# A gated sum of an FFT filter and a Mish layer on one core: first x tiles moved up, small dummy products, the plain rows of W in two transfers, and a new order

## The chip, the cores and the metric

The kernel runs on one core of a Trainium2 chip. A core has TensorE (PE, matrix products into PSUM), VectorE (DVE), ScalarE (ACT), GpSimd (POOL) and SyncE (SP, here the issuer of nearly all DMA transfers), and 16 DMA engines that carry the transfers. The metric is the device time of one execution in microseconds, the median of several runs.

## The reference: what is computed

`x` is 2048 x 512. Two branches read it, and a gate per row mixes them:

```python
g = sigmoid((x * gate_w).sum(-1, keepdims=True))
a = irfft2(rfft2(x) * (w_r + 1j * w_i), s=(2048, 512))     # w: 2048 x 257
h = x @ w1 + b1                                            # w1: 512 x 1792
b = (h * tanh(softplus(h))) @ w2                           # Mish, w2: 1792 x 512
out = g * a + (1 - g) * b                                  # bf16
```

## The kernel before, in words

`x` is held as 16 tiles of 128 rows (row `16 p + t` is partition `p` of tile `t`). Both branches are written as products with a 128 x 128 or 128 x 512 moving side on TensorE.

*The dense branch.* It needs `x` transposed. Tiles 0 to 7 are transposed by TensorE (`tr0` to `tr7`, line 562) and copied out of PSUM (`evx`); tiles 8 to 15 by transposing DMAs (`xt8` to `xt15`, line 462). The rows go in four chunks c of four tiles. `m{c}_{ft}` (line 866) is a group of four products of 512 columns for one of 14 slices of w1; ACT applies Mish as it empties the bank (`h{c}_{ft}`, line 871). `n{t}` (line 884) is 14 products with w2 for tile t; `o{t}` scales it by 1 - g.

*The FFT branch*, a chain of products with constant matrices: sum and difference of the halves of x (`bf`, line 575, DVE or POOL), `p0` to `p15` (line 588) with evacuations `ep`, `d0` to `d15` (line 603) with `ed`, then a re-layout through 16 SBUF-to-SBUF transfers `s{fq}_{r}` (rE<-rD), then `t{q}_{i}` (line 718, needs `s` of its quarter and the constants `ldM`) with evacuations `et`. The filter is `p1`, `p2`, `ad` on DVE with copies `sw` (swapped halves); a correction of the edge frequencies (`e1`, `xp`, `es`, `ead`, `e2`, `e3`); the inverse chain `it`, `eit`, eight transfers `hx`, `id`, `ec`, `ey`, and `ip`, `fin`, which add it to the other branch. `gate0`, `gate8`, `zcl`, `ez`, `omg`, `zt` and the like compute the gate.

*The weights W of the filter.* For the real part (`wr`) and the imaginary part (`wi`) the 2048 x 257 rows go into the staging tile `rS`. The frequencies are paired with their mirror images: plain rows go forward (`wr0s0`, `wr1s0`, `wi0s0`, `wi1s0`, 16 runs of 16,448 bytes each), mirrored rows one by one backward (`...s1`, runs of 514 bytes; `...s2` a single row of each). The copies `wrm...`, `wim...` (lines 644, 645), `wrn`, `win`, `wrc`, `wrz` (and `wi...`) unfold them into `rW` and `rA`. `rS` is later reused for Mish results of chunk 3.

*The order.* Nothing loops: each step is a task, and the string `ORDER` (line 326) lists all tasks. An entry is name, engine where there is a choice, and buffer numbers (PSUM banks or `tmp` slots). Each engine issues its tasks strictly in that order; `emit` puts the semaphore waits ahead of each instruction. The DMA tasks are SP's, and SP issues them in order as well (`braw`, `graw` and the last output are on ACT's queue). A task that waits holds all that stand behind it on its engine. The string came from a planner that used the durations given with the tasks (the numbers in `dma(...)` and `G.add(...)`); at run time these numbers do nothing.

*The start.* `warm` (line 509) is 13 products of 256 columns on a constant, with no input. The bytes of the first transfers decide when `tr`, `bf`, `p` and the first `m` can run.

Of the kernel before, what the change touches and what calls it, by code (L numbers as in the profile page):

```python
# [346 lines left out]
ec0:dve:0 id3 n0_0::7 ec2:act:1 ey0_0 ey0_1 ey2_0 ey2_1 id4::4 o0_0:act ip0::0 id10::2 id11 ip1::1 fin0 ec10:act:1 id14::6 id15 id5 fin1 ec14:act:0
n6_0::0 ec4:act:2 ey10_0 out1 ey14_0 ey14_1 ey10_1 ey4_1 id8::6 o6_0:act id9 id6::2 ey4_0 n11_0::1 ec8:act:1 ey8_1 ey8_0 ip3::0 ip11_0 fin3 id7
o11_0:act n14_0::6 ec6:act:1 ey6_1 ey6_0 ip7::7 ip14_0 id12::2 o14_0:dve n4_0::1 out14 ip6::6 o4_0:act n10_0::0 fin6 ip10_0 ip2::6 o10_0:act ip4::1
fin2 n7_0::4 out11 fin4 out3 n15_256::6 o7_0:act fin7 ip15_256 id13 out7 o15_256:act n8_0::7 ec12:dve:1 out15_256 ey12_1 ey12_0 ip8_0 n13_0::6 o8_0:act  # L350
ip13_0 n12_0::7 o13_0:act ip12_0 n9_0::6 o12_0:act out13 ip9_0 ip5::7 o9_0:act n15_0::2 fin5 out9 out5 ip15_0 o15_0:act out15_0
"""


def _build(nc, A_x, A_w_r, A_w_i, B_x, B_w1, B_b1, B_w2, gate_w, out, merge=8, xtp=8, NWARM=13):
# [4 lines left out]
    d_M = nc.inline_tensor(_bf16_bits(cs["M"]), name="c_m").bitcast(BF)  # L360
    d_G = nc.inline_tensor(_bf16_bits(cs["G"]), name="c_g").bitcast(BF)
    scz = nc.dram_tensor("scz", (NT, 128), BF)

    G = _Graph(3)
    es = ExitStack()
    with es:
# [61 lines left out]
        def bank(b, i=0):  # L428
            return ps[:, b.slot + i, :]
# [27 lines left out]
        def dma(name, dst, src, us, cls="dma", queue="sp", is_out=False, transpose=False, **kw):  # L457
            def fn(e, _dst=dst, _src=src):
                a = _dst() if callable(_dst) else _dst
                b = _src() if callable(_src) else _src  # L460
                if transpose:
                    return e.dma_start(a, b, transpose=True)  # L462
                return e.dma_start(a, b)  # L463
# [40 lines left out]
        wb = _Buf("b1")  # L504
# [467 lines left out]
```

## Time and profile before

| | us |
|---|---|
| median of 3 runs (range) | 137.81 (137.18 to 137.94) |
| the profiled execution's time | 137.92 |
| its span, first to last instruction | 136.2 |
| TensorE (PE) busy | 127.2 (93%) |
| DVE, ACT, POOL busy | 77.6, 76.7, 13.1 |
| bytes moved | 20.41 MB, 150 GB/s over the span |

The page names groups of instructions by line, engine, operation and tile; "idle before" is the time in which the engine had nothing to run just before an instruction, with what ended it. `PEclk` and the clock column of a table of windows give the granted clock of TensorE as a share of full speed. The columns of such a table are: the stretch, its length, busy time of PE, PEld (weight loads), DVE, ACT and POOL with the number of instructions, the clock, the share of time that the 16 DMA engines were busy, and GB/s. In lists of waits the numbers are us in total, times, and the longest. A DMA line gives how many issues, KB each, and us from issue to landing; a queue line gives packets, MB, and share of the 16 engines' time. A timeline line gives start, length, engine, line, operation, tiles and count; lines on SP are the time that it takes SP to issue.

### The profile page before, as it was taken

The numbers are of one execution on the slowest core, as the hardware profiler recorded it, in microseconds if no ns is written. First come the engines' busy times: TensorE is split into PE (matmuls) and PEld (weight loads), VectorE is DVE, ScalarE is ACT, GpSimd is POOL, SyncE is SP. The second block draws the span as 40 slices with busy tenths as digits, with TensorE's granted clock in tenths as the row PEclk, the third lists the DMA queues.
The fourth block names the chain that finished last, engine by engine and source line by source line (L and its number), as shares of the span: only waits on it lengthen the run. The fifth ranks groups of instructions, "written<-read, shape, count | busy, mean of one in ns | idle before, by whom it ended". The sixth has DMA issues, their size and how long they took to land.

```text
span 136.2 us, 2309 instructions
## 1 busy us (share of the span) xinstructions
PE 127.2 (93%) x902; PEld 71.2 (52%) x918; DVE 77.6 (57%) x129; ACT 76.7 (56%) x107; POOL 13.1 (10%) x21
## 2 busy tenths in 40 slices
PE   7499999999998699999989999999999999999992
PEld 5295577654564255444536664466554444744451
DVE  0474669575699989998952458036975224340020
ACT  4067889897798789999977910232433022312221
POOL 3032045403400000000040000000000000000000
PEclk9959999999999999999999999999999999999999
DMA  4999999996876899579923100780200102220024
GB/s 119 317 244 278 162 379 240 331 146 149 197 172 136 182 170 207 114 236 346 386 79 104 56 0 0 279 338 2 82 0 0 39 0 80 79 96 0 0 77 173
DMA packets 15710, 20.41 MB, mean 150 GB/s; under 512 B 5780, under 2 KB 11796, under 8 KB 15636
## 3 DMA queue, kind: packets, MB, share of 16 engines
q1 hardware_dynamic: 15520, 20.20, 55.3%
q8 instruction: 7, 0.11, 0.4%
q10 hardware_dynamic: 180, 0.07, 0.2%
q14 instruction: 3, 0.02, 0.1%
HBM read 12.92 MB, written 2.10 MB: 110 GB/s over the span
## 4 chain that ended last, share of the span: by engine, by line
PE 56%; ACT 13%; SPq 12%; DMA 11%; DVE 3%; issue 2%; POOLq 1%
PE ps L884 35%; SPq L463 10%; PE ps L866 10%; DMA rS<-in_A_w_r_dram 8%; DMA rX<-in_A_x_dram 3%; ACT rD L871 3%; ACT rW L665 3%; PE ps L840 3%; PE ps L796 3%; ACT rD L496 2%; SPq L462 2%; ACT hs L871 2%; DVE rC L742 1%; PE ps L892 1%; PE ps L910 1%
## 5 line engine op out<-in xcount | busy, mean ns | idle before, releaser
L866 PE MATMUL ps<-rX,w_sb 128*128 128x512 bf16 x215 | 50.9, 380 | 2.0 <-DMA rX<-in_A_x_dram 1.2
L866 PEld LDWEIGHTS ps<-rX,w_sb 128*128 128x128 bf16 x224 | 20.9, 98 | 23.4 <-issue 2.1
L898 ACT ACTIVATE rX<-ps,omg 128x512 bf16<-128x512 f32 (+1 forms) x14 | 9.2, 657 | 42.3 <-PE ps L884 23.8
L884 PE MATMUL ps<-w_sb,hs 128*128 128x512 bf16 x108 | 24.8, 379 | 0.2
L871 ACT ACTIVATE hs<-ps,b1f 128x512 bf16<-128x512 f32 x28 | 18.9, 690 | 3.0 <-PE ps L866 2.7
L914 DVE SCALAR_TENSOR_TENSOR rX<-ps,gcol,rX 128x512 bf16<-128x512 f32 x8 | 5.8, 748 | 21.5 <-PE ps L910 17.9
L884 PEld LDWEIGHTS ps<-w_sb,hs 128*128 128x128 bf16 x112 | 10.7, 98 | 12.1
L884 PE MATMUL ps<-w_sb,rS 128*128 128x512 bf16 (+1 forms) x70 | 12.9, 336 | 0.0
L496 ACT ACTIVATE rC<-ps 128x1024 bf16<-128x1024 f32 x12 | 12.2, 1032 | 1.1 <-PE ps L718 0.7
L884 PE MATMUL ps<-w_sb,rD 128*128 128x512 bf16 x53 | 12.3, 379 | 0.2
L851 DVE TENSOR_TENSOR rA<-tmp,ps 128x512 bf16<-128x512 f32 x16 | 10.0, 682 | 1.1 <-ACT tmp L847 1.1
L871 ACT ACTIVATE rS<-ps,b1f 128x512 bf16<-128x512 f32 x14 | 9.3, 697 | 1.9 <-PE ps L866 1.9
L871 ACT ACTIVATE rD<-ps,b1f 128x512 bf16<-128x512 f32 x14 | 9.1, 692 | 1.7 <-PE ps L866 1.6
L884 PEld LDWEIGHTS ps<-w_sb,rS 128*128 128x128 bf16 x70 | 6.8, 98 | 5.5
L884 PEld LDWEIGHTS ps<-w_sb,rD 128*128 128x128 bf16 x56 | 5.4, 98 | 6.1
L575 DVE TENSOR_TENSOR rB<-rA 128x1024 bf16<-128x1024 bf16 (+1 forms) x8 | 4.8, 637 | 6.3 <-DMA rA<-in_A_x_dram 6.3
L728 DVE COPY tmp<-rC 64x1024 bf16<-64x1024 bf16 x15 | 6.2, 421 | 1.6 <-ACT tmp L729 0.7
L588 PE MATMUL ps<-w_sb,rB 128*128 128x128 bf16 x64 | 5.5, 246 | 0.1
L493 DVE CAST rC<-ps 128x1024 bf16<-128x1024 f32 x4 | 4.9, 1218 | 1.3 <-PE ps L588 0.7
L493 DVE CAST rF<-ps 128x1024 bf16<-128x1024 f32 x4 | 4.7, 1218 | 1.3 <-PE ps L796 1.3
L742 DVE TENSOR_TENSOR rC<-rC,tmp 128x1024 bf16<-128x1024 bf16 x8 | 5.3, 688 | 0.1
L496 ACT ACTIVATE rX<-ps 128x512 bf16<-128x512 bf16 x4 | 2.4, 595 | 5.3 <-PE ps L562 5.3
(84 smaller groups left out, 133.6 us busy)
## 6 DMA issues: line engine op xcount, KB each, us to landing
w_sb<-in_B_w_dram SPq DMA_DIRECT2D x3, 768.0 KB, 9.7
rF<-c_m SPq DMA_DIRECT2D x4, 512.0 KB, 13.7
rE<-rD SPq DMA_DIRECT2D x16, 128.0 KB, 2.3
rB<-c_g SPq DMA_DIRECT2D x4, 512.0 KB, 7.1
out_dram<-rX SPq DMA_DIRECT2D x7, 256.0 KB, 2.1
rA<-in_A_x_dram SPq DMA_DIRECT2D x3, 512.0 KB, 7.6
rC<-rF SPq DMA_DIRECT2D x4, 384.0 KB, 3.0
w_sb<-in_B_w_dram SPq DMA_DIRECT2D x2, 512.0 KB, 9.5
```

Of the source, the lines that this page charges most:

```text
L463: return e.dma_start(a, b)
L493: return e.tensor_copy(out=o(), in_=i())
L496: return e.activation(o(), i(), AF.Copy)
L588: ins = e.matmul(bank(b, i)[:, 128 * c:128 * (c + 1)], xu[:, t, uv, e_:256:2], RF, start=True, stop=True)
L728: G.add(f"sw{q}_{j}", [("dve", 0.37, lambda e, z=z, lo=lo, i_=i_: e.tensor_copy(out=tb(z)[lo:lo + 64], in_=i_)), ("act", act(1024), lambda ...
L742: return e.tensor_tensor(out=Y[:, fa:fb, :], in0=Y[:, fa:fb, :], in1=zv(z), op=ALU.add)
L851: return e.tensor_tensor(out=yb[:, t:t + 2, 256 * h:256 * h + 256].rearrange("p t (i e) -> p t i e", e=2), in0=t4(z), in1=o4(bank(b, 1)), ...
L866: ins = e.matmul(bank(b), w1_sb[:, dt_, 128 * ft:128 * (ft + 1)], xT[:, c, dt_, :, :], start=(dt_ == 0), stop=(dt_ == 3))
L871: G.add(f"h{c}_{ft}", [("act", act(512, 1), lambda e, c=c, ft=ft, b=b: e.activation(hs[c][:, ft, :], bank(b), AF.Mish, bias=b1f[:, ft:ft + ...
L884: ins = e.matmul(bank(b)[:, 0:hi - lo], hs[c][:, ft, 128 * tl:128 * (tl + 1)], w2_sb[:, ft, lo:hi], start=(ft == 0), stop=(ft == NFT - 1 a ...
L898: return e.activation(bs[:, t, lo:hi], bank(b)[:, 0:hi - lo], AF.Copy, scale=omg[:, t:t + 1])
L914: return e.scalar_tensor_tensor(out=bs[:, t, :], in0=bank(b), scalar=gcol[:, t:t + 1], in1=bs[:, t, :], op0=ALU.mult, op1=ALU.add)
```

## The change

Four things, and a new `ORDER` for all tasks:

- The transfer of tiles 0 and 1 (`x0`) is the first on SP, `x2` the second; `x4` was first.
- 14 new tasks `fl0` to `fl13`, each two products of 128 columns on the same constant and PSUM bank as `warm`, without inputs; they stand among the first transposes and `p` products.
- The plain rows of W come in one transfer for each of `wr` and `wi` (`wrs0`, `wis0`) of 32 rows of 16,448 bytes, to every second partition of 64, in place of two of 16 rows each. The mirrored rows stay as they were.
- Some planner durations of DMA tasks are other numbers.

Lines after the insertion are 8 higher than before (562 becomes 570, 718 becomes 726, 866 becomes 874).

```diff
 ORDER = """
-warm::0 braw wrp1 x4 ones lut ident wrp0 cRF ebase graw x0 w1_0 tr7::0 bf4_1:dve x2 tr4::1 bf4_0:dve tr5::2 wi0s0 evx4:dve tr0::3 bf0_1:pool evx5:dve
-tr_b::1 evx7:dve p6::4 evx0:act wr0s2 p7 ev_b p4::6 bf0_0:dve tr6::3 x12 ep6:dve p5 evx6:act p0::0 p1 tr1::2 ep4:act m1_3::3 ep0:dve bf2_0:pool x8
-evx1:act tr2::6 m1_1::7 h1_3 bf2_1:dve wr0s0 evx2:act p2::2 p3 h1_1 tr3::6 m1_0::0 ep2:act evx3:dve wr0s1 bf12_0:dve m0_3::1 h1_0 bf12_1:dve m1_2::2
-h0_3 bf8_0:dve w1_4 bf8_1:dve p14::6 h1_2 p15 p12::0 m0_0::3 wip1 ep14:act wip0 cFD p8::4 ldM2 h0_0 p9 gate0::6 ep8:act wrm010:dve p13 p10::2 ldM1 zcl0
-wrm000:pool ep12:dve p11 m0_2::4 ep10:act m0_7::5 wi0s1 h0_2 wrm001:dve d4::2 h0_7 d5 d10::0 wrm011:dve d11 ed4:act d0::6 ldM3 d1 ed10:dve m0_6::5 ez0
-ed0:act d2::2 m1_4::4 ldM0 wrn0:dve h0_6 m1_7::6 h1_4 ez10 w1_8 wrc0:dve d3 omg0 wrz0:pool h1_7 d8::4 ezb0 gc0 d9 m1_6::7 ed2:act d6::0 ed8:act d7
-m0_4::6 wi0s2 ed6:dve h1_6 xt12 d14::4 d15 h0_4 d12::2 d13 ed14:act m1_5::0 ed12:dve xt9 m0_5::1 h1_5 wim001:dve s0_1 m1_10::2 h0_5 wim011:dve s3_2
-m0_9::3 wim010:dve s0_3 h1_10 s0_2 m1_8::1 wim000:pool h0_9 s0_0 m1_12::0 h1_8 s1_1 s2_1 m0_8::3 h1_12 win0:dve s2_3 m1_11::2 h0_8 s1_3 t1_0::0
-wic0:pool s1_0 h1_11 t1_1 t0_0::4 wiz0:pool et1:dve s1_2 t0_1 m0_10::3 et0:act xt10 m0_13::2 sw1_0:dve:0 h0_10 sw0_0:dve:1 s3_1 m0_11::4 sw0_1:dve
-h0_13 sw1_1:dve s2_0 p2_0:dve t3_0::0 h0_11 t3_1 s2_2 t2_0::2 p2_1:dve t2_1 et3:act m1_9::5 xt8 p1_1:dve et2:act p1_0:dve m0_12::4 xt11 sw3_1:dve:2
-h1_9 t4_0::0 ad_0:dve t4_1 t5_0::2 h0_12 t5_1 sw3_0:dve m1_13::5 s3_0 sw2_1:dve:1 et5:act sw2_0:dve s3_3 m0_1::4 p1_3:dve et4:act wr1s1 p1_2:dve
-m2_6::2 h0_1 p2_2:dve h1_13 m2_8::3 wr1s0 p2_3:dve h2_6 ad_2:dve t7_0::4 m2_2::0 h2_8 wi1s0 ad_3:dve sw4_0:dve:1 t7_1 h2_2 m2_12::3 sw4_1:dve wi1s1
-sw5_0:dve:2 et7:act m2_1::2 sw5_1:dve ad_1:dve h2_12 t6_0::4 m2_0::0 sw7_0:dve:0 h2_1 ldG3 wrm111:dve t6_1 h2_0 m2_3::2 sw7_1:dve wrm100:dve rft
-et6:act m2_10::3 wrm101:dve xt14 h2_3 m2_7::4 wrm110:dve h2_10 xt15 wim110:dve wrn1:act m2_11::5 wim100:dve m2_13::3 xt13 wim111:dve m2_5::2 wim101:dve
-w2_8 m2_4::0 win1:dve m2_9::1 h2_11 wrc1:dve h2_4 wic1:dve inv m3_8::6 h2_9 wiz1:dve wrz1:pool ldG0 p1_5:dve m3_4::5 h2_13 p1_4:dve h3_8 ldG1 m3_2::3
-p2_4:dve h2_7 p2_5:dve m3_7::6 h3_4 edge ad_4:dve h3_2 m3_1::7 p2_7:dve w2_2 sw6_0:act:1 p1_7:dve m3_11::3 h3_1 sw6_1:dve m3_13::5 ad_7:dve h3_11
-p1_6:dve ldG2 h2_5 m3_3::7 p2_6:dve h3_13 gate8::2 h3_3 ad_5:dve h3_7 m3_9::3 ad_6:dve zcl8 e1::6 ez8 m3_10::2 h3_9 xp1::1 ezb8 es0::2 ez18 zt::3
...
+warm::0 lut ebase x0 ones wrp1 x2 wrp0 ident braw cRF graw w1_0 fl0 fl1 fl2 fl3 bf0_1:dve tr1::1 ldM2 tr0::2 bf0_0:dve evx1:act fl4 fl5 evx0:dve fl6
+fl7 bf2_0:pool tr3::3 fl8 tr_b::2 fl9 evx3:act p0::4 ev_b p1 x4 tr2::1 bf2_1:dve ep0:act fl10 fl11 fl12 evx2:dve fl13 p2::2 p3 m0_3::1 ep2:act w1_4
+m0_2::0 h0_3 m0_0::2 h0_2 ldM0 m0_1::3 h0_0 bf4_0:dve cFD tr4::0 bf4_1:dve h0_1 tr6::1 tr7::2 x12 tr5::4 evx4:dve p6::6 evx7:dve p7 m0_5::0 evx6:dve
+ep6:act evx5:dve x8 p4::2 p5 h0_5 m1_7::6 ep4:act ldM1 m1_1::7 h1_7 m1_5::2 h1_1 bf12_1:dve w1_8 m1_4::3 bf12_0:dve h1_5 gate0::7 h1_4 bf8_0:dve p14::0
+bf8_1:dve p15 p12::2 zcl0 ep14:act p13 wrs0 wip0 p10::4 p11 ez0 p8::6 ep12:act p9 m1_3::0 ez10 wip1 ep8:dve wr0s1 ep10:act m1_2::1 omg0 ezb0 h1_3 gc0
+d0::4 d1 h1_2 d10::6 d11 wi0s1 d8::2 ed0:act m0_13::0 ed10:act m1_12::1 h0_13 wr1s1 d4::4 d5 d6::6 h1_12 ed4:dve d7 d9 ed6:act m1_8::0 wr0s2 d14::4
+ed8:act d15 d12::6 xt10 ed14:dve d13 m1_10::1 h1_8 ed12:act d2::2 xt11 d3 m1_0::0 ed2:act wrm111:dve m0_9::6 xt9 h1_10 wrm001:dve h1_0 m0_4::7
+wrm000:dve h0_9 s0_3 m1_9::0 wrm011:dve h0_4 s0_1 wrm110:dve m0_10::1 s2_2 h1_9 wrm100:dve s1_0 m1_13::7 h0_10 s1_3 wrm101:pool m0_11::6 s1_2 h1_13
+s0_0 m1_6::1 h0_11 s2_3 wrn1:dve m0_12::0 s1_1 h1_6 s3_1 m0_7::6 h0_12 wrc1:dve s3_2 m0_8::7 wrm010:pool wrz1:dve h0_7 s0_2 t2_0::0 s2_0 h0_8 t3_0::2
+t3_1 xt8 t2_1 et3:act m0_6::6 et2:dve t1_0::4 s3_3 sw3_0:act:0 t1_1 t0_0::2 wrn0:dve t0_1 s2_1 m1_11::7 et0:act s3_0 et1:dve m2_6::0 wi1s1 h1_11
+sw2_0:act:1 m2_12::1 sw3_1:dve sw0_1:dve:2 h0_6 t4_0::4 sw2_1:dve ldM3 t5_0::2 t5_1 wrc0:dve h2_6 m2_9::7 et5:dve wrz0:pool h2_12 p1_3:pool t4_1 wis0
+h2_9 m2_4::0 et4:dve sw0_0:act m2_1::1 h2_4 wi0s2 p1_0:dve m2_10::4 h2_1 xt13 p1_2:dve m2_2::5 h2_10 xt15 t7_0::0 h2_2 t7_1 m2_0::4 et7:act wim111:dve
+xt12 t6_0::6 t6_1 wim010:dve wim110:act m2_3::5 wim101:dve xt14 m2_7::0 wim001:dve m2_13::1 et6:act wim011:dve ldG0 wim100:dve m2_5::2 wim000:act w2_8
+win1:dve m2_8::3 m3_0::6 h2_13 win0:dve h2_3 gate8::7 h3_0 ldG2 wic1:dve m3_8::5 h2_0 zcl8 wiz1:dve ez8 h2_7 m3_5::7 wic0:dve h2_5 w2_2 ez18 wiz0:dve
+m3_10::4 omg8 h3_5 p2_2:dve h3_8 m3_12::2 p2_3:dve h3_10 ad_2:dve m3_9::5 h3_12 ad_3:dve ldG1 sw1_0:act:1 m3_3::4 ezb8 sw7_1:dve:0 p2_0:dve sw1_1:act
+zt::2 m3_13::7 edge zte ad_0:dve sw7_0:act m3_11::2 inv p1_1:dve rft h3_9 m3_6::6 p2_1:dve zw sw5_1:act:2 p1_7:dve m3_7::5 ldG3 ad_1:dve h3_3 m3_4::0
+sw5_0:dve h3_7 p2_7:dve h3_13 w2_0 m3_1::1 p1_5:dve h3_4 zr ad_7:dve m3_2::7 h3_1 p2_5:dve h3_6 m2_11::0 sw6_1:dve:0 h3_2 ad_5:dve h3_11 sw4_0:dve:1
...
 """
...
+        for i in range(NFILL):
+            def f_fill(e):
+                ins = None
+                for _ in range(2):
+                    ins = e.matmul(bank(wb)[:, 0:128], one, one, start=True, stop=True)
+                return ins
+
+            G.add(f"fl{i}", [("pe", 0.112, f_fill)], "fl", writes=[wb])
...
         for ri, (src, nm) in enumerate(((A_w_r, "wr"), (A_w_i, "wi"))):
             wv = src.rearrange("(q m) k -> q m k", m=128)
+            dma(f"{nm}s0", rS[64 * ri:64 * ri + 64:2, :], src.rearrange("(q g m) k -> g q (m k)", g=4, q=16)[0:2], 1.6, writes=[(nm, 0, "s", 0), (nm, 1, "s", 0)])
             for fh in range(2):
                 sg = stg[64 * ri + 32 * fh:64 * ri + 32 * fh + 32]
                 c0_ = 1 - fh
-                parts = [(0, slice(0, 32), slice(32 * fh, 32 * fh + 32), 1.2),
-                         (1, slice(c0_, 32), slice(127, 96, -1) if fh == 0 else slice(96, 64, -1), 1.8)]
+                parts = [(1, slice(c0_, 32), slice(127, 96, -1) if fh == 0 else slice(96, 64, -1), 2.0)]
                 if fh == 0:
                     parts.append((1, slice(0, 1), slice(64, 65), 0.15))
                 for j, (pm, fs, ms, us) in enumerate(parts):
-                    dma(f"{nm}{fh}s{j}", sg[pm:32:2, fs, :], wv[:, ms, :], us, writes=[(nm, fh, "s", j)])
+                    dma(f"{nm}{fh}s{j + 1}", sg[pm:32:2, fs, :], wv[:, ms, :], us, writes=[(nm, fh, "s", j + 1)])
```

More of the change, by code (lines that the diff above doesn't have):

```diff
@@ L343 @@
-p1_6:dve ldG2 h2_5 m3_3::7 p2_6:dve h3_13 gate8::2 h3_3 ad_5:dve h3_7 m3_9::3 ad_6:dve zcl8 e1::6 ez8 m3_10::2 h3_9 xp1::1 ezb8 es0::2 ez18 zt::3
-m3_5::7 omg8 es1 zte h3_10 xp2 zw m3_0::6 ead::0 h3_5 e2::2 m3_6::7 h3_0 e3 w2_0 it4_0::2 h3_6 it4_1 zr it2_0::4 it2_1 eit4:act m3_12::6 eit2:dve
-it0_0::0 h3_12 it0_1 it3_0::2 it3_1 eit0:act it6_0::4 it6_1 n5_0::6 eit6:act rfs eit3:act it1_0::2 o5_0:dve it1_1 it5_0::4 it5_1 eit1:dve it7_0::0
-it7_1 n2_0::6 eit7:dve eit5:dve n1_0::7 hx0_01 o2_0:dve hx4_11 hx0_11 hx0_10 hx0_00 n3_0::6 hx4_01 o1_0:act hx4_00 hx4_10 id0::4 o3_0:act id1 id2::0
@@ L347 @@
[L347 to L350, printed above, removed]
@@ L351 @@
-ip13_0 n12_0::7 o13_0:act ip12_0 n9_0::6 o12_0:act out13 ip9_0 ip5::7 o9_0:act n15_0::2 fin5 out9 out5 ip15_0 o15_0:act out15_0
+warm::0 lut ebase x0 ones wrp1 x2 wrp0 ident braw cRF graw w1_0 fl0 fl1 fl2 fl3 bf0_1:dve tr1::1 ldM2 tr0::2 bf0_0:dve evx1:act fl4 fl5 evx0:dve fl6
+fl7 bf2_0:pool tr3::3 fl8 tr_b::2 fl9 evx3:act p0::4 ev_b p1 x4 tr2::1 bf2_1:dve ep0:act fl10 fl11 fl12 evx2:dve fl13 p2::2 p3 m0_3::1 ep2:act w1_4
+m0_2::0 h0_3 m0_0::2 h0_2 ldM0 m0_1::3 h0_0 bf4_0:dve cFD tr4::0 bf4_1:dve h0_1 tr6::1 tr7::2 x12 tr5::4 evx4:dve p6::6 evx7:dve p7 m0_5::0 evx6:dve
@@ new lines @@
+zt::2 m3_13::7 edge zte ad_0:dve sw7_0:act m3_11::2 inv p1_1:dve rft h3_9 m3_6::6 p2_1:dve zw sw5_1:act:2 p1_7:dve m3_7::5 ldG3 ad_1:dve h3_3 m3_4::0
+sw5_0:dve h3_7 p2_7:dve h3_13 w2_0 m3_1::1 p1_5:dve h3_4 zr ad_7:dve m3_2::7 h3_1 p2_5:dve h3_6 m2_11::0 sw6_1:dve:0 h3_2 ad_5:dve h3_11 sw4_0:dve:1
+sw4_1:dve n2_0::1 h2_8 p2_4:dve h2_11 p1_4:dve sw6_0:act rfs p2_6:dve p1_6:dve n3_0::0 o2_0:act ad_4:dve ad_6:dve e1::1 n6_0::3 o3_0:act xp1::0 es0::1
+es1 xp2 ead::2 e2::2 n1_0::1 o6_0:act e3 it0_0::2 o1_0:dve it0_1 it6_0::6 eit0:act it6_1 it5_0::4 it5_1 it1_0::0 eit5:dve eit6:act it1_1 n0_0::2
@@ new lines @@
+eit1:act it7_0::0 o0_0:dve it7_1 it2_0::4 eit7:act it2_1 it4_0::6 eit2:dve it4_1 it3_0::2 eit4:act it3_1 n5_0::0 eit3:dve hx0_11 hx0_01 hx0_00 n7_0::1
+o5_0:act hx0_10 hx4_10 hx4_11 hx4_00 id2::2 o7_0:act id3 id0::6 id1 ec2:act:2 hx4_01 n4_0::0 ec0:act:0 ey2_1 ey0_0 ey2_0 ey0_1 ip2::1 o4_0:act ip1::6
+fin2 ip0::7 id14::2 id15 fin1 id10::4 ec14:act:0 ip3::1 id11 fin3 ey14_0 n15_0::0 out3 ec10:dve:2 ip15_0 o15_0:act ey14_1 n14_0::6 out15_0 ey10_1
+ey10_0 fin0 out1 id4::4 id5 id12::2 ec4:act:2 id13 ip14_0 id6::0 ec12:act:0 ey4_0 id7 n10_0::7 o14_0:act ey4_1 out14 ec6:dve:1 ey12_1 ey6_0 ey6_1
@@ L352, with _build @@
+ip10_0 ip4::6 ey12_0 n13_0::4 o10_0:dve fin4 n12_0::5 ip13_0 ip5::6 o13_0:act id8::2 fin5 ip7::7 ip12_0 id9 o12_0:dve ip6::4 out5 ec8:act:0 n11_0::6
+fin6 out13 ey8_0 ey8_1 fin7 n8_0::2 out7 ip8_0 ip11_0 o8_0:act n9_0::7 o11_0:act out11 ip9_0 n15_256::6 o9_0:dve out9 ip15_256 o15_256:act out15_256
 """
-def _build(nc, A_x, A_w_r, A_w_i, B_x, B_w1, B_b1, B_w2, gate_w, out, merge=8, xtp=8, NWARM=13):
+def _build(nc, A_x, A_w_r, A_w_i, B_x, B_w1, B_b1, B_w2, gate_w, out, merge=8, xtp=8, NWARM=13, NFILL=14):
@@ L526, in _build @@
         for a, b_ in ((0, 4), (4, 8), (8, 14)):
-            dma(f"w1_{a}", w1_sb[:, :, 128 * a:128 * b_], w1v[:, :, 128 * a:128 * b_], 0.4 * (b_ - a),
+            dma(f"w1_{a}", w1_sb[:, :, 128 * a:128 * b_], w1v[:, :, 128 * a:128 * b_], 0.44 * (b_ - a),
                 writes=[("w1", f) for f in range(a, b_)])
@@ L617, in _build @@
         for g in range(4):
-            dma(f"ldM{g}", Mm[:, 16 * g:16 * g + 16, :], d_M[:, 16 * g:16 * g + 16, :], 1.4, writes=[("M", g)])
+            dma(f"ldM{g}", Mm[:, 16 * g:16 * g + 16, :], d_M[:, 16 * g:16 * g + 16, :], 1.5, writes=[("M", g)])
         for g in range(4):
-            dma(f"ldG{g}", Gm[:, 16 * g:16 * g + 16, :], d_G[:, 16 * g:16 * g + 16, :], 1.4, writes=[("G", g)], deps=t_p)
+            dma(f"ldG{g}", Gm[:, 16 * g:16 * g + 16, :], d_G[:, 16 * g:16 * g + 16, :], 1.5, writes=[("G", g)], deps=t_p)
         t_mv = []
@@ L827, in _build @@
         for a, b_ in ((2, 8), (8, 14), (0, 2)):
-            dma(f"w2_{a}", w2_sb[:, a:b_, :], w2v[:, a:b_, :], 0.36 * (b_ - a), writes=[("w2", f) for f in range(a, b_)],
+            dma(f"w2_{a}", w2_sb[:, a:b_, :], w2v[:, a:b_, :], 0.42 * (b_ - a), writes=[("w2", f) for f in range(a, b_)],
                 deps=[t_trb] + t_p + t_d + t_zw if a == 0 else [])
```

## The prediction

> **What bounds the kernel now.** I read the page's busy shares first, then TensorE's waits, the clock by window, the SyncE (SP) queue's timeline, and the DMA queues. From the page:
>
> ```profile
> span 136.2 us, 2309 instructions
> ...
> PE 127.2 (93%) x902; PEld 71.2 (52%) x918; DVE 77.6 (57%) x129; ACT 76.7 (56%) x107; POOL 13.1 (10%) x21
> ...
> DMA  4999999996876899579923100780200102220024
> ...
> q10 hardware_dynamic: 180, 0.07, 0.2%
> ```
>
> TensorE (PE) is busy 93% of the span: a change is worth what it does to TensorE's gaps and clock. The DMA engines are full for the first 30 us (digits of 9), so what lands when is decided there by the order of issue. TensorE's waits, over the span:
>
> ```profile
> PE ps L562 <- DMA rA<-in_A_x_dram: 1.8, 2, 1.4
> PE ps L866 <- DMA rX<-in_A_x_dram: 1.2, 1, 1.2
> PE ps L509 <- PEq L957: 0.8, 1, 0.8
> PE ps L817 <- DVE ezb L701: 0.7, 1, 0.7
> PE ps L718 <- ACT rC L496: 0.5, 1, 0.5
> ```
>
> x tiles cost 1.8 us at the start, a transposed x tile (xt11) 1.2 us before chunk 2, zt 0.7, a PSUM bank 0.5. Then the windows with TensorE's clock:
>
> ```profile
> 4.00:7.44 3.44, 1.74 (x24) 1.39 (x25) 2.27 (x6) 0.60 (x1) 0.79 (x1) 1.00 1.09 350
> 7.44:10.85 3.41, 3.19 (x30) 2.99 (x28) 2.68 (x6) 2.00 (x3) 1.29 (x2) 0.50 0.95 243
> ```
>
> After a stretch in which TensorE was busy 1.74 of 3.44 us, the clock is 0.50 for 3.41 us: up to 1.6 us lost. Timeline of SP, and of TensorE where it needs what SP issued:
>
> ```profile
> 12.05 4.83 SPq L463 DMA_DIRECT2D rF<-c_m  x2
> ...
> 19.59 5.57 SPq L462 DMA_TRANSPOSE rX<-in_A_x_dram  x2
> ...
> 30.51 6.92 SPq L463 DMA_DIRECT2D rE<-rD  x11
> ...
> 35.90 1.06 PE L718 MATMUL ps<-rE,rF 128*128 128x128 bf16 x16
> ```
>
> Two issues of 0.43 us each took 4.83 us, two transposing ones of 1.27 us took 5.57: SP is held while seven or eight transfers are outstanding, and everything behind waits with it. The sixteen re-layout transfers (s tasks, rE<-rD) go out at 0.63 us each, land 2.3 us later and feed the t products (L718). Last, the queue of the ACT issues, from 1.9 to 4.2 us and from 134 us on:
>
> ```profile
> q10 hardware_dynamic: 36, 0.00, 1.3%
> ```
> ```profile
> q10 hardware_dynamic: 144, 0.07, 10.2%
> ```
>
> The first holds two transfers, of 14 rows (bias) and 4 rows (gate): 18 data packets, and 18 of 4 bytes, one per DMA engine used: 14 and 4. The second is one transfer of 128 rows: 128 and 16. So a transfer's outermost count sets over how many of the 16 engines it is spread: 4 rows got 4 engines.
>
> **The change part by part.** The profiled execution took 137.92 us, 0.11 over the median (137.81) and 1.72 over its span; I add 1.72 to spans.
>
> *Tiles 0 and 1 first.* x4 (512 KB), first in line, landed 4.34 us after its issue at 0.81; the DMA engines moved 6.7 MB between its landing at 5.15 and that of w1_8 at 30.25, 0.267 MB/us. x0 has half the bytes, 1.0 us less: 4.1 to 5.1. I take 4.9; TensorE starts 0.3 us earlier (0 to 1.0). Behind it x4 is now fifth: 2.1 MB at 0.267 after 3.2 (5.15 less x4's own 2.0) gives 11, and TensorE needs it then: x0's and x2's transposes and p products are 64 times 56 ns, m0_3, m0_2, m0_0, m0_1 are 4 times 0.86, and w1_0 lands near 7.5. So it is about even until 11.
>
> *Fourteen dummies.* 28 products of 128 columns, 56 ns each at full clock (24 d products took 1.34): 1.6 us. Eight fit before x0 lands; 20 (1.1 us) stand between transposes, where TensorE waits for DVE anyway. They raise the busy share of the window from 51% to some 75%. If the 0.50 window goes, up to 1.6 us; but TensorE then waits for x4 instead, so I take 0.7 (between 0 and 1.6), and nothing for the dummies (they could cost 1.1).
>
> A rule weighed: the Trainium skill, TensorE: Matmul & The Clock Gate, section "Why this matters for your kernels", asks for no idle gap over about 3 us. The longest gap here was 1.4 us and the clock still halved, so by the rule the dummies would be worth 0, by the row up to 1.6.
>
> *New order, rest.* xt9, xt10, xt11 go ahead of the s transfers: the 1.2 us wait goes. The 0.5 at t4 and 0.6 of zt's 0.7 go too, if t and ezb are as early as now. New small waits at zt, m3_11, m3_7, m3_2 by DVE's longer list: some 0.5. Tail (2.6 us after the last product) unchanged. Sum: 136.2 - 0.3 - 0.7 - 1.2 - 0.5 - 0.6 + 0.5 = 133.4, call it 133.7 with half of a dummy cost. That is the span if the W transfers are as quick as now. LdM3, wi1s1 and wis0 are behind the s transfers, with slack then.
>
> *Plain rows of W in two transfers.* Four of 16 rows (16,448 bytes a row) become wrs0 and wis0, 32 rows each. The saving of two issues (1.2 us of SP) is off the path. But the source is written `"(q g m) k -> g q (m k)"[0:2]`: its outermost count is 2, where the destination's is 32. The trace has no transfer whose sides differ so. Bounds: 16 engines, 2 rows each, or 2 engines, 16 rows each. The 64 such packets took 1,156 ns in the median, 692 at the least. So 1.4 to 2.3 us, or 11.1 to 18.5 us. I take the second, since in the ACT queue's rows the outermost count gave the engines, and a cut of both sides at their outermost index can't make more than 2 pieces here; 0.75 us a row, near the least, since 14 engines then read little beside it: 12 us.
>
> The Trainium skill, DMA: Bandwidth & Descriptors, section "Why a DMA increments its semaphore by 16 and not by 1", says that the count of engines is the largest up to 16 that divides both sides' slowest dimension: 2 here. It agrees with the 14, 4 and 16 of the ACT queue. By its 27 GiB/s an engine, a transfer would be 9.1 us (an estimate), and the sum some 6 us lower than mine.
>
> What queues behind: on SP wrs0 comes after 5.65 MB, so its rows begin at 3.2 + 5.65/0.267 = 24 and end at 36. Each later transfer uses all engines, so its share on those two waits: wr0s1 (now 18.4 after 16.84: 1.54 us), wi0s1, wr1s1: to 40.7. SP is held as at 12.05 and 19.59: xt10 goes out when wrs0 is through, xt11 and xt9 behind the next ones, s0_3 near 40.7, s1_1 (eight issues later, 5.1 us) at 45.8, landing 48. DVE meets wrm111 (needs wrs0, wr1s1) at about 33 and stands there until 41; behind it queue all W copies and the evacuation et2. TensorE reaches t2_0 at about 41: 4.9 + 160 products of 56 ns (9.0) + gate 0.8 + 26 mm1 groups of 0.86 (22.4) + dummies 1.1 + 3 of half clock and waits. It waits about 7 us (3 if SP is not held, 13 at 1,156 ns a row).
>
> Then xt8 and the other s transfers, wi1s1, ldM3: wis0 starts on its engines near 58, ends at 70. ACT stands at wim110 until then, with et6 behind it; t6's bank and xt12 to xt15 (queued behind wis0) hold m3_0 until 73. Without the narrow transfers m3_0 would be reached at 58 (41 + 3.6 of t + 15 groups of 0.86 = 57.5). Delay at m3_0: 15 us; it holds the first wait and its half clock. After an idle stretch of some 7 us another 3.41 us at 0.50: 1.7. Sum: 133.7 + 15 + 1.7 = 150.4, plus 1.72: 152.1; I say 151.5.
>
> **The rivals.** (1) *W spreads over all engines.* For it: destinations' outermost count is 32, and every 257 KB transfer of before used all 16. Span 133.7: 135.4 us, faster by 1.7%; 133.4 to 137 by the front's terms. (2) *Narrow, but partly covered*: rows at 0.69 us and SP not held. For it: the W products are DVE's, off TensorE's path until the edge step; against it: the s and xt transfers share the two engines. t2_0 then waits 3 to 4, m3_0 is late by 9: 133.7 + 9 + 1.7 + 1.7 = 146; down to 142 if xt12 to xt15 come 4 us earlier still. (3) *W spreads, and the front is slower*: x4 and w1_4 land 2 us later than reckoned, TensorE waits, the dummies cost 1.1: 133.7 + 3 = 136.7, so 138.4. Against it: the four mm1 groups of w1_0 cover 3.4 us. It decides from 13 us on for x4's landing.
>
> **How the numbers follow.** A difference under 0.5% can't be told from none. Narrow in full: 0.55, 148 to 165; narrow and partly covered: 0.18, 142 to 148; spread and faster: 0.20; spread and slower front: 0.07, of it 0.04 within 0.5% and 0.03 slower. Faster 0.20, same 0.04, slower 0.76. Likeliest case's own range 146 to 163. For 8 in 10 the range must reach into the spread case: 135.2 to 163.
>
> **What the profile after would show.** If right: TensorE waits of several us at L726 (t) near 41 to 48 and at L874 near 65 to 73; DVE idle some 8 us before an L653 TENSOR_SCALAR on rS, ended by a DMA; a DMA digit low (2 engines of 16 are 0.1) from about 25 to 36 and again from 58; wrs0's landing near 29 us after its issue at 8. If the clock reckoning is right: PEclk without a 5 in the third slice, but with 5s after both long waits. Wrong if wrs0 lands near 26 and t starts at 41 without a wait: then the engines were 16. Wrong also if the narrow transfers run but SP is never held: then the second half of the delay shrinks.

## The result, and the profile after

The changed kernel takes 155.62 us (median of 4 runs, 153.56 to 157.74); the kernel before took 137.84 beside it. The ratio is 1.121, 95% interval 1.112 to 1.129: slower by 12%. Times here and below are medians of all runs of a kernel, while ratios are of its fast runs alone (those within 1.5% of its quickest, here 153.56 and 154.97). The prediction said 151.5, and 135.2 to 163 as the range. The profiled execution of the changed kernel, at 157.74 us (span 156.0), is the longest of the four, so a wait read from it can be a few us above the typical one.

The page of the kernel after, with the lines that answer to those of before:

```profile
span 156.0 us, 2376 instructions
...
PE 132.6 (85%) x946; PEld 73.8 (47%) x946; DVE 74.6 (48%) x127; ACT 82.8 (53%) x112; POOL 12.2 (8%) x18
...
PE   7999999999149960009999999999999999999992
...
PEclk9999999999978999555899999999999999999999
DMA  3899987148995991139990350000028222003112
```

TensorE has the work of before and the dummies (132.6 us busy against 127.2, part of it at half clock), and it has two holes, in the slices near 40 and near 60 us. Its waits name them:

```profile
PE ps L726 <- DMA rF<-c_m: 12.8, 1, 12.8
PE ps L726 <- DMA rE<-rD: 5.5, 1, 5.5
PE ps L509 <- PEq L965: 0.8, 1, 0.8
```

Both end at a `t` product (L726): the first waits for the re-layout transfers `s` (rE<-rD), the second for the constants `ldM3` (rF<-c_m). The waits of before for x tiles, `xt11`, `zt` and a PSUM bank are gone or 0.3 us. The timeline of SP in the kernel after shows what held the first:

```profile
8.76 1.89 SPq L463 DMA_DIRECT2D rS<-in_A_w_r_dram  x2
...
14.36 17.92 SPq L463 DMA_DIRECT2D rS<-in_A_w_r_dram  x2
32.32 5.24 SPq L462 DMA_TRANSPOSE rX<-in_A_x_dram  x3
37.69 8.19 SPq L463 DMA_DIRECT2D rE<-rD  x13
...
52.89 16.68 SPq L462 DMA_TRANSPOSE rX<-in_A_x_dram  x4
```

`wrs0` is the first of the two issues at 8.76. Two later issues (`wr1s1`, `wr0s2`) took 17.92 us until SP came to the x transposes at 32.32 and to the first `s` at 37.69; the same happened behind `wis0`, where four transposes took 16.68. By the semaphores, `wr0s1` got 14 of its 16 updates between 19.57 and 24.66 us and the last two at 34.62 and 36.16, when the rows of `wrs0` were through: its shares on two engines had waited. In the trace the 32 rows of `wrs0` ran from 17.33 to 34.45 us, those of `wis0` from 55.30 to 69.17. DVE stood meanwhile at the first copy of the mirrored rows (timeline of DVE):

```profile
37.60 0.70 DVE L653 TENSOR_SCALAR rW<-rS 32x2064 bf16<-32x2064 bf16 x1 [7.95 <-DMA rS<-in_A_w_r_dram]
```

The windows of the kernel after around the two holes (length, busy PE, PEld, DVE, ACT, POOL, then clock, DMA share, GB/s):

```profile
41.35:44.76 3.41, 0.00 (x0) 0.00 (x0) 1.31 (x2) 0.00 (x0) 1.90 (x1) 1.00 0.91 206
44.76:48.17 3.41, 2.99 (x20) 2.19 (x21) 1.89 (x4) 1.48 (x2) 1.91 (x1) 0.50 0.80 179
58.42:61.83 3.41, 0.00 (x0) 0.00 (x0) 0.00 (x0) 0.00 (x0) 0.00 (x0) 1.00 0.12 34
61.83:68.65 6.82, 0.00 (x0) 0.00 (x0) 0.00 (x0) 0.00 (x0) 0.00 (x0) 0.50 0.14 42
68.65:75.48 6.83, 5.40 (x25) 3.06 (x26) 5.42 (x7) 4.28 (x4) 0.00 (x0) 0.50 0.94 247
```

From 58 to 68 us none of the compute engines does anything at all, and the DMA share is 0.12 to 0.14: 2 of 16 (0.125) carry `wis0`, at 34 to 42 GB/s. The other 14 are held rather than free: fourteen of the 16 completions of `ldM3` come only from 69.65 us on. The view counts a packet where it begins, and 25 packets of 256 and 4 bytes that began between 55.17 and 56.04 us all end at 69.6, just after the last row (the last section has more on this). And the clock stays at 0.50 for a while after each hole.

The list of DMA issues (how many, KB each, median us to landing), of the kernel before and then of the one after:

```profile
rS<-in_A_w_r_dram SPq DMA_DIRECT2D x3, 257.0 KB, 4.8
```
```profile
rS<-in_A_w_r_dram SPq DMA_DIRECT2D x1, 514.0 KB
rS<-in_A_w_i_dram SPq DMA_DIRECT2D x1, 514.0 KB
```

The two new transfers have no landing time, because the view looks for 16 updates of a semaphore. Theirs got three in the trace, one 1.1 us after the issue and two at the end, at 33.98 and 35.04 for `wrs0`; their rows run two at a time. So two engines carried the data.

### The profile page after: what moved, and what is told of

Its sections match the earlier page's. It is cut to its first block, busy times and chain, and to the rows that moved or that the text cites. A ratio compares the mean times of both kernels' runs of the same rounds, so it can differ in the third digit from the quotient of the medians.

```text
span 156.0 us, 2376 instructions
## 1 busy us (share of the span) xinstructions
PE 132.6 (85%) x946; PEld 73.8 (47%) x946; DVE 74.6 (48%) x127; ACT 82.8 (53%) x112; POOL 12.2 (8%) x18
## 4 chain that ended last, share of the span: by engine, by line
PE 55%; DMA 22%; SPq 12%; ACT 4%; DVE 2%; issue 1%; POOLq 1%
PE ps L892 31%; PE ps L874 14%; DMA rF<-c_m 12%; SPq L463 12%; DMA w_sb<-in_B_w_dram 10%; PE ps L804 2%; PE ps L848 2%; ACT tmp L737 2%; ACT rS L879 2%; PE ps L611 2%; PE ps L726 1%; PE ps L900 1%; PE ps L918 1%; POOLq L304 1%; SPq L462 1%
## 5 line engine op out<-in xcount | busy, mean ns | idle before, releaser
L874 PE MATMUL ps<-rX,w_sb 128*128 128x512 bf16 x224 | 54.1, 393 | 0.6 <-DMA w_sb<-in_B_w_dram 0.3
L906 ACT ACTIVATE rX<-ps,omg 128x512 bf16<-128x512 f32 (+1 forms) x12 | 7.7, 652 | 31.8 <-PE ps L900 20.6
L496 ACT ACTIVATE rC<-ps 128x1024 bf16<-128x1024 f32 x11 | 11.2, 1040 | 22.4 <-PE ps L726 19.9
L726 PE MATMUL ps<-rE,rF 128*128 128x128 bf16 x64 | 6.2, 265 | 18.4 <-DMA rF<-c_m 12.8
L879 ACT ACTIVATE hs<-ps,b1f 128x512 bf16<-128x512 f32 x28 | 18.8, 693 | 2.4 <-PE ps L874 2.1
L726 PEld LDWEIGHTS ps<-rE,rF 128*128 128x128 bf16 x64 | 5.4, 122 | 20.7 <-issue 20.1
L892 PE MATMUL ps<-w_sb,rS 128*128 128x512 bf16 (+1 forms) x70 | 12.7, 336 | 0.0
L909 DVE TENSOR_SCALAR rX<-ps,omg 128x512 bf16<-128x512 f32 x5 | 3.7, 747 | 11.7 <-PE ps L900 6.9
L879 ACT ACTIVATE rS<-ps,b1f 128x512 bf16<-128x512 f32 x14 | 8.5, 696 | 1.5 <-PE ps L874 1.4
L737 ACT ACTIVATE tmp<-rC 64x1024 bf16<-64x1024 bf16 x8 | 8.4, 1055 | 0.3
L653 DVE TENSOR_SCALAR rA<-rS 32x2064 bf16<-32x2064 bf16 x3 | 2.1, 703 | 12.7 <-DMA rS<-in_A_w_i_dram 12.7
L496 ACT ACTIVATE rF<-ps 128x1024 bf16<-128x1024 f32 x5 | 4.8, 1023 | 4.8 <-PE ps L804 4.8
## 6 DMA issues: line engine op xcount, KB each, us to landing
rF<-c_m SPq DMA_DIRECT2D x4, 512.0 KB, 11.1
```

Source lines behind the costliest of these rows:

```text
L496: return e.activation(o(), i(), AF.Copy)
L726: ins = e.matmul(bank(b, i)[:, 128 * k:128 * (k + 1)], Mm[:, f, :], In[:, f, :], start=True, stop=True)
L737: ("act", act(1024), lambda e, z=z, lo=lo, i_=i_: e.activation(tb(z)[lo:lo + 64], i_, AF.Copy))],
L874: ins = e.matmul(bank(b), w1_sb[:, dt_, 128 * ft:128 * (ft + 1)], xT[:, c, dt_, :, :], start=(dt_ == 0), stop=(dt_ == 3))
L879: G.add(f"h{c}_{ft}", [("act", act(512, 1), lambda e, c=c, ft=ft, b=b: e.activation(hs[c][:, ft, :], bank(b), AF.Mish, bias=b1f[:, ft:ft + ...
L892: ins = e.matmul(bank(b)[:, 0:hi - lo], hs[c][:, ft, 128 * tl:128 * (tl + 1)], w2_sb[:, ft, lo:hi], start=(ft == 0), stop=(ft == NFT - 1 a ...
```

## The experiments

My theory: `wrs0` and `wis0` run on 2 of the 16 DMA engines, since their source's outermost count is 2; every later transfer has a share on those two, so it waits as well, and SP with it. Rivals: the new order or the dummies carry the loss; only the W copies' own wait for the rows matters; the single large transfer is slow for another reason.

**Back to four transfers of W, all else as changed.**

```diff
-            dma(f"{nm}s0", rS[64 * ri:64 * ri + 64:2, :], src.rearrange("(q g m) k -> g q (m k)", g=4, q=16)[0:2], ...)
+            for fh in range(2):
+                dma(f"{nm}{fh}s0", stg[64 * ri + 32 * fh:64 * ri + 32 * fh + 32:2, :, :], wv[:, 32 * fh:32 * fh + 32, :], ...)
```

In `ORDER`, `wrs0` becomes `wr1s0 wr0s0` and `wis0` becomes `wi1s0 wi0s0`.

> The changed kernel, new order and dummies and all, with the plain rows of W in four transfers of 16 rows again (wr1s0, wr0s0 in wrs0's place, wi1s0, wi0s0 in wis0's). Theory (the two-row outermost count puts each W transfer on 2 of the 16 engines): both long waits of TensorE go (5.5 us at t2_0, 12.8 us at t7_0), the spans falls to 132 to 136 us, the time to 134 to 138 us. Rival (the new order itself, with the s transfers and ldM3 late in SP's queue, makes the waits): time stays above 148 us.

137.41 us, ratio to the kernel before 1.0014 (0.9968 to 1.0061). TensorE's longest waits:

```profile
PE ps L509 <- PEq L966: 0.8, 1, 0.8
PE ps L727 <- DMA rF<-c_m: 0.7, 1, 0.7
PE ps L875 <- DMA w_sb<-in_B_w_dram: 0.4, 1, 0.4
```

Both holes are gone. The whole loss is the two transfers': 18.2 us by the medians, 12% or some 16 us by the ratios (1.121 against 1.001). The new order, tiles 0 and 1 first and dummies together change nothing that can be measured, where 1.7% was reckoned.

**Only one of the two narrow**: `wr` in one transfer and `wi` in two (label e2), and the other way round (e3).

> The changed kernel with only wrs0 in the narrow form; the imaginary part in four-transfer form (16 rows each). Theory: the wait of 5 to 6 us before t2_0 stays, with one stretch of half clock (1 to 2 us); the one before t7_0 goes; time 141 to 144 us. Rival (waits are the order's): both stay, above 150 us.

> The changed kernel with only wis0 in the narrow form; the real part in transfers of 16 rows. Theory: no wait at t2_0; wis0 goes out some 5 us earlier, its rows take 14 to 17 us, so TensorE's wait at t7_0 stays, 10 to 14 us, with 2 to 3 us of half clock: time 147 to 152 us. Together with the one before, the two losses over four transfers should add up to the whole, 18 to 21 us. Rival (waits are the order's): both waits stay, above 150 us, with one at t2_0.

141.93 us (ratio 1.036, 1.026 to 1.045) and 151.75 us (1.107, 1.093 to 1.122). The first wait of each, by the lists of waits of e2 and of e3:

```profile
PE ps L730 <- DMA rE<-rD: 2.5, 1, 2.5
```
```profile
PE ps L730 <- DMA rF<-c_m: 12.3, 1, 12.3
```

Against four transfers they lose 4.5 and 14.3 us, 18.8 together; both at once lost 18.2. By the ratios it is 3.4% and 10.6%, 14.0% together, against 11.9%. The losses add up as far as two runs of each can tell (the intervals are 1.0 to 1.5% to either side). The first wait was 2.5 rather than the 5 to 6 I expected: `s1_1` landed 1.1 us earlier (43.97 instead of 45.09), and TensorE came to `t2_0` at 41.5 instead of 39.6, held up ahead of it by 1.4 for w1 and 0.9 for DVE.

**The kernel before with the narrow transfers alone**, in its old order (`wr0s0` replaced by `wrs0`, `wi0s0` by `wis0`, `wr1s0` and `wi1s0` dropped).

> The kernel before, its order kept, with the two narrow W transfers alone: wis0 in wi0s0's place (sixth on SP), wrs0 in wr0s0's (tenth), wr1s0 and wi1s0 gone. Theory (2 engines, 14 to 17 us a transfer, all later transfers wait on those two): x12 and x8 land after 22 us in place of 12 and 16, w1_4 near 38 in place of 19.6; TensorE waits 15 to 25 us in the first 45 us: 150 to 163 us. Rival (a transfer of 32 rows is no slower than two of 16; the new order is at fault): 136 to 139 us.

162.17 us (one run). The waits there:

```profile
PE ps L588 <- DVE rB L575: 11.9, 1, 11.9
PE ps L866 <- DMA w_sb<-in_B_w_dram: 8.7, 1, 8.7
```

In the old order the W transfers are ahead of x tiles and of a part of w1, so it is those that come late: the same two transfers, other victims. It was more than with the new order.

**Without the dummies**, four W transfers (e1 with `fl0` to `fl13` taken out of `ORDER`), and **the kernel before with the dummies alone**.

```diff
-tr7::0 ... tr0::3 ... tr_b::1
+fl0 fl1 fl2 fl3 fl4 fl5 tr7::0 ... fl6 fl7 fl8 fl9 tr0::3 ... fl10 fl11 fl12 fl13 tr_b::1
```

> The new order with W in four transfers of 16 rows (137.41 us with the dummies), now without the 14 dummies. The profile of that kernel shows the dummies at 2.7 us of TensorE between 4 and 8 us, and a wait of 0.39 us for w1_0 at 8.78 behind them. Theory A, the dummies stand in TensorE's path: 1 to 2 us less, 135.4 to 136.4, and no wait over 1 us takes their place. Theory B, they keep the clock up, as the prediction reckoned (0.7 us, at most 1.7): a 3.4 us stretch at 0.50 comes back in the front and the time is 138.1 to 139.1. Theory C, w1_0's landing (8.7 us) sets when the first products of W1 start, whatever stands ahead: a wait of 1.5 to 3 us for w_sb ends near 8.8 in the profile, and the time is 137 to 138. I hold C likeliest.

> The kernel before with only the 14 dummies added, 6 ahead of the transposes of x4's tiles, 4 ahead of those of x0's first, 4 ahead of that of the bias. The prediction's step: the 0.50 window between 7.44 and 10.85 goes and is worth 0.7 us, up to 1.6, with nothing for the dummies: ratio 0.988 to 0.995. Rival: the window is worth nothing, since what TensorE does there waits for DVE and DMA anyway, and the dummies cost 0 to 1 us where they stand between transposes: ratio 1.000 to 1.008. Runs of the kernel before whose mean clock was 1.000 were no quicker (136.1 to 138.9 us) than those at 0.987 (136.6 to 136.9), which speaks for the rival.

Without the dummies: 139.63 us, ratio 1.019 (1.013 to 1.025), against 1.0014 with them. That is B's number, but not B's reason: the clock of the profiled run was 1.000 throughout. The place was C's:

```profile
PE ps L875 <- DMA w_sb<-in_B_w_dram: 1.6, 1, 1.6
PE ps L849 <- issue: 1.1, 1, 1.1
```

With the dummies TensorE started the first `m` group at 8.78 us, after a wait of 0.39 for `w1_0`; without them at 9.03, after 1.62. So the dummies mostly fill a wait for `w1_0`, and only 0.25 us of the 2.2 is there. Set side by side, the kernel without them is 1.2 us behind at `m0_13` (a wait behind evacuations on ACT near 25 us), 0.8 at `id2`, and 2.0 from `id14` on, where the transfer `hx4_00` landed 5.4 us after its issue (4.3 with the dummies, 3.3 in e9 below). Two fetches of instructions, 16,384 and 8,192 bytes, ran on the DMA engines at 100.5 and 101.4 us there, in the middle of those transfers; with the dummies only the smaller fell among them. That is read from three traces and was not tried apart, so why the dummies are worth 2 us in this order stays open.

Dummies alone in the kernel before: 137.16 us, ratio 0.9996 (0.995 to 1.004): the rival's result. In its profiled run the clock does not fall in the front, but at 20.0 us, again for 3.41 us at 0.50; 11 of its 13 runs have a mean clock of 0.999 or more, so no such window. Nor have most runs of the kernel before without dummies: 33 of the 43 in these sessions have 0.998 or more, where the profiled one had 0.987. So the 0.7 us reckoned for the window are not to be had by the dummies.

**The narrow transfers on ACT's queue.**

```diff
-            dma(f"{nm}s0", rS[64 * ri:64 * ri + 64:2, :], ..., 1.6, writes=...)
+            dma(f"{nm}s0", rS[64 * ri:64 * ri + 64:2, :], ..., 1.6, queue="act", writes=...)
```

> The changed kernel with the two narrow transfers issued by ACT on its own queue, at their places in ACT's order; all else as it is (155.62 us). If the loss comes from the two DMA engines alone (rows of all queues in one line): every transfer's share on those two still waits, and the waits before t2_0 and t7_0 stay at 4 to 6 and 10 to 13 us, 152 to 157 us. If it comes from the queue (transfers of SP's queue wait behind the rows only because they are in the same queue, and SP is held since they are outstanding): wr0s1, wi0s1, wr1s1, xt10 and ldM3 land within 3 us of their issue, SP's issues of over 5 us go, and what is left is the wait of the W copies for the rows themselves: 141 to 149 us.

165.64 us (ratio 1.210, 1.198 to 1.222), outside both ranges. The waits and SP's issues:

```profile
PE ps L874 <- ACT rC L496: 13.4, 1, 13.4
PE ps L726 <- DMA rE<-rD: 12.7, 1, 12.7
```
```profile
30.79 17.01 SPq L463 DMA_DIRECT2D rE<-rD  x13
```

What I had not reckoned with is ACT's order: it issued `wrs0` at 19.48 us instead of 8.76 and `wis0` at 59.43 instead of 51.64, so the rows ended at 43.46 and 80.65. For the question asked, it speaks for the engines: `xt10`, issued at 19.07 on the other queue, landed at 43.94, `xt11` at 45.99, and 13 issues of `s` took 17.01 us (8.19 in the changed kernel) while the rows ran. Behind `wis0`, a load of weights (`w_sb`) that SP issued at 60.69 got 14 of its 16 updates by 69.36 and the last two at 81.71 and 82.97, after the rows. Another queue does not get past the rows.

**`ldM3` ahead of the re-layout transfers.**

```diff
-xt9 h1_10 ... sw2_1:dve ldM3 t5_0::2
+xt9 ldM3 h1_10 ... sw2_1:dve t5_0::2
```

> The changed kernel with ldM3 moved ahead, right behind xt9 and before the 16 re-layout transfers; all else as it is (155.62 us, second wait 12.8 us at t7_0, ended by ldM3's last completion at 69.8). The prediction's step: without ldM3 in the way TensorE runs on to m3_0, whose bank is freed by et6, behind wim110 on ACT, which stands until wis0 has landed near 70: the wait moves there, is 8 to 12 us, and the time stays within 152 to 156. Rival: ldM3 was the whole of the second wait, and the rows of wis0 are hidden once it is out of the way: second wait under 3 us, 141 to 146 us.

154.12 us (ratio 1.126, 1.113 to 1.138). The waits, and the timeline of ACT:

```profile
PE ps L726 <- DMA rE<-rD: 7.9, 1, 7.9
PE ps L874 <- ACT rC L496: 4.2, 1, 4.2
```
```profile
67.23 1.93 ACT L650 ACTIVATE rA<-rS 32x2064 bf16<-32x2064 bf16 x1 [5.40 <-DMA rS<-in_A_w_i_dram]
69.18 1.02 ACT L496 ACTIVATE rC<-ps 128x1024 bf16<-128x1024 f32 x1
```

`t7_0` no longer waits. TensorE runs on to `m3_0` and waits there until 70.35: ACT stands at `wim110` for the rows of `wis0`, then runs `et6` (69.18), which frees the bank. This is the wait that the prediction named. It is 4.2 us, not the 8 to 12 I gave it, and the first wait is 7.9, since `ldM3`'s 512 KB are now ahead of the `s` transfers. The second wait moved and got shorter, and yet the time stayed (1.126 against 1.121): behind it the clock was 0.50 for 10.24 us, from 68.57 to 78.81, and the first wait was longer.

**The outermost count itself: 16, and 4.**

```diff
-src.rearrange("(q g m) k -> g q (m k)", g=4, q=16)[0:2]
+src.rearrange("(q g m) k -> q g (m k)", g=4, q=16)[:, 0:2]     # label e9
+src.rearrange("(a b m) k -> a b (m k)", a=4, b=16)[:, 0:8]     # label e10
```

> The changed kernel with one thing altered: the source of wrs0 and wis0 is taken as (q, g) instead of (g, q), so that its outermost count is 16, not 2; still one transfer each of 32 rows of 16,448 bytes to 32 of 64 partitions, at the same places on SP. The rows of W land in another order, so this part of the output is not the reference's; the amount of work is the same. Theory, the outermost count of both sides sets how many DMA engines a transfer uses: all 16 engines, 2 rows each, the semaphores get 16 updates, no wait over 1.5 us at t2_0 and t7_0, 136.4 to 138.4 us like the kernel with four transfers (137.41). Rival, it is the single transfer of 32 long rows over 64 partitions itself that is slow: 152 to 157 us as before this edit. Between them (139 to 145 us) would say that both have a part.

> As the one above, but with an outermost count of 4 in the source (4 groups of 8 rows; other rows of W than the reference's, the same amount). Theory: 4 engines, 8 rows each, 7 to 8.6 us of rows at 0.87 to 1.07 us a row, semaphores with few updates that come from 4 engines. wrs0 would then end near 26, where the four transfers ended too (25.7), so the first wait is under 1.5 us; wis0's rows end near 63 instead of 69, and the second wait is 4 to 7 us instead of 12.8. In all 141 to 146 us. If the loss went with the rows an engine has to do and nothing were hidden, half of the 18.2 us: 146 to 148. If the outermost count is not the cause: 152 to 157.

With 16: 137.0 us, ratio 0.995 (0.990 to 0.9995). With 4: 144.86 us, ratio 1.043 (1.028 to 1.057). The DMA issues and the longest waits of e9, then of e10:

```profile
rS<-in_A_w_r_dram SPq DMA_DIRECT2D x1, 514.0 KB, 17.7
rS<-in_A_w_i_dram SPq DMA_DIRECT2D x1, 514.0 KB, 7.5
```
```profile
PE ps L874 <- DMA w_sb<-in_B_w_dram: 2.5, 2, 1.5
PE ps L509 <- PEq L965: 0.8, 1, 0.8
```
```profile
rS<-in_A_w_i_dram SPq DMA_DIRECT2D x1, 514.0 KB
```
```profile
PE ps L726 <- DMA rF<-c_m: 6.8, 1, 6.8
```
```profile
52.00:54.00 2.00, 0.00 (x0) 0.00 (x0) 0.00 (x0) 0.85 (x2) 0.00 (x0) 1.00 0.22 70
```

The same number of bytes, in single transfers as before, to the same partitions: with 16 the landing is whole again and neither hole is left; with 4 the second wait is 6.8 us, half of 12.8, the DMA share is 0.22 from 52 to 54 us, where nearly nothing but the rows begins, near 4 of 16 (0.25), and the semaphores got five updates, one early and four at the end (16 with an outermost count of 16). `wis0` took 13.9 us of rows with 2 engines, 8.1 with 4, 3.8 with 16. This settles the cause. Neither is a kernel to keep: both put other rows of W where the reference wants them, and the gain of 0.5% with 16 is at the edge of what the runs can tell.

The Trainium skill, DMA: Bandwidth & Descriptors, section "Why a DMA increments its semaphore by 16 and not by 1", has the engines as the largest count up to 16 that divides both sides' slowest dimension. The runs agree for 2, 4 and 16 against 32. By the 27 GiB/s an engine of the page's section "Specifications", a row of 16,448 bytes would be 0.57 us on one engine (an estimate); the quickest here took 0.61, and the mean of 16 in a line was 0.87 to 1.07 in the changed kernel.

## Why the prediction was right, point by point

- *Narrow, 2 engines of 16 rows*: right, by the DMA share of 0.12 to 0.14, three semaphore updates, and e9 and e10. It was read from the ACT queue's 14, 4 and 16 data packets, where no two sides were known to differ; that the smaller side decides was a choice there, held at 0.73, and the runs bear it out.
- *0.75 us a row, 12 us a transfer*: too low. `wrs0` took 17.1 us (1.07 a row), `wis0` 13.9 (0.87), inside the 11.1 to 18.5. The step said that 14 engines would then read little beside it. For `wrs0` that failed: other transfers' shares ran among its rows, from 17.3 on rather than from 24. The two errors nearly cancel: rows ended at 34.5, 36 was said.
- *The queue behind `wrs0`*: right. `wr0s1` landed at 36.16, `wi0s1` 36.67, `wr1s1` 37.50 (40.7 said), `xt10` went out at 32.32, `s0_3` at 37.69 (40.7), `s1_1` landed at 45.09 (48). DVE stood 7.95 us, to 37.6 (33 to 41 said). TensorE came to `t2_0` at 39.6 (41) and waited 5.5 (7 said; 2.5 in e2, 7.9 in e8). All 1.4 to 3.4 us early, with the right links. One reading did not hold: that SP is held "while seven or eight transfers are outstanding". Here it stood with four outstanding (24.27 to 32.28 us) and with five (55.66 to 67.11); what sets the limit stays open.
- *The second wait*: its cause right, its place and size not. It was 12.8 us and ended at 70, where some 8 (65 to 73) were said, and it was not at `m3_0` but at `t7_0`. The step said that `ldM3` had slack there. It was issued at 50.95, before `wis0`; its first completions came at 55.61, its last at 69.83, after the rows. e8 shows that the wait the prediction named stood behind this one.
- *1.7 us of half clock after a long wait*: too little. The window after the first hole was 0.50 for 3.41 us (TensorE at work for 3.0 of it), as reckoned within the delay of 15. Behind the second, for which the 1.7 was added, it was 0.50 from 61.83 to 75.48, and TensorE worked at it for 5.4 us: 2.7 lost (half of 5.4, an estimate).
- *The front*: `x0` landed at 3.92 (4.9 taken; just outside the 4.1 to 5.1 given), the transposes began at 4.15 in place of 5.19, `x4` landed at 11.18 (11 said; TensorE waited 0.3), and the third slice has no 5.
- *Rival 1's sum, 135.4*: the spread case was 137.41. Of its terms, the waits for `xt11`, for the bank at `t4` and most of `zt`'s went as said. What failed is "I take 0.7" for the clock and "nothing for the dummies". In e1 the 28 products took 3.1 us of TensorE, not 1.6, 2.7 of them between 4 and 8 us, since the span begins at half rate (last section); `w1_0` landed there at 8.64, not at 7.5, and the start of the first `m` group at 8.78 hangs on it. (It landed at 8.3 to 9.5 in all eight experiments with this front; the 6.85 in the changed kernel's own profile is the exception.) The dummies alone in the kernel before brought nothing. The "half of a dummy cost" that was added is 0.3, not half of 1.1. The sum was also made against a profiled 137.92, while the medians of before in the sessions of e1 and e5 were 136.99 and 137.23.
- *Rivals 2 and 3*: not this one, with rows at 0.87 to 1.07 us and SP held; e10 with 4 engines is what rival 2's 142 to 148 looks like. Nor rival 3: `x4` landed 2 us before the point from which it decides.

So the prediction had 135.4 for the order without the narrow transfers and 16.7 for these, 152.1, and said 151.5. The first term measured 137.4 (e1), 2.0 more; the second 16 to 18. That the second fits so well is partly luck: the rows were longer than taken (5 us for `wrs0`, hidden by its earlier start, 2 for `wis0`) and so was the half clock (1.0), while the first wait was 1.5 shorter.

## What to carry to other kernels

Merging two transfers into one can cost engines: look at the outermost count of both sides of a DMA, not at the bytes or at the partitions reached, and see in the trace whether its semaphore gets 16 updates. In these traces a transfer on few engines held all that were issued behind it and even what was issued just before it, on other queues too, so it is priced by the rows of one engine in a line and by every wait behind it. Transposing transfers right behind it may have made that worse (not tried apart). Here, saving two issues of 0.6 us cost 16 to 18.

## What was not expected of the hardware

- A transfer issued *before* the narrow one can end after it: `ldM3`, issued 0.7 us ahead of `wis0`, had its first completions at 55.61 and its last at 69.83. The same in e3 (51.50 and 65.32) and, with 4 engines, in e10 (50.14 and 58.45); 48.54 and 50.86 with four transfers. This is not the wait of two shares that `wr0s1` shows: of `ldM3`'s 16 completions two came by 55.66 and fourteen from 69.65 on. What differs is that transposing transfers followed at once, and the packets that stood from 55 to 69.6 us are mostly of 256 bytes, the size in which those go. Such packets stand up to 12.7, 12.3 and 7.2 us in e3, e8 and e10. Where no transposes were outstanding (`wr0s1`, the loads behind `wis0` in e7, the x tiles in e4), 14 completions came early and two late. So it looks, in six traces, as if transposes whose shares on the busy engines wait hold up the other engines too; no run tried the same order without them.
- The clock comes back in steps of 3.41 us counted from the start of the fall, not from the moment TensorE works again: four such steps from 61.83 to 75.48, of which TensorE worked the last 5.4 us; five in e7 (73.36 to 90.42), two in e10 (56.85 to 63.68).
- A span begins at half rate, for a time that differs by execution. In e1 the dummies and the transposes beside them followed each other every 107 ns up to 5.8 us, as products do in the 0.50 window of the kernel before, and then every 55 to 60 ns; in the changed kernel's profile that came at 3.8 us, in e9's at 4.5. So 28 dummies took 3.1 us in e1.
- Instruction fetches of 16,384 bytes, seven in a span, took 0.9 to 2.0 us each on a DMA engine in e1, e5 and e9. Where they fell among small transfers that TensorE waits for, those landed later (5.4 us for `hx4` in e5, 3.3 in e9, where none fell among them); this is read from three traces and was not tried apart.
